# The operations of the attention and Fourier part in a written-out order

## The chip, the cores and the metric

The kernel runs on one core of a Trainium2 chip. The time is that of one execution on the device, in microseconds (us), measured without the profiler over several runs; their median counts. One more execution was recorded by the profiler, and all rows below are from it.

## The reference

For 8 batches of 8 heads, 576 positions and 64 features a head, a linear attention is computed without a softmax, then normalized; the result is reordered to `x` of 8 x 576 rows of 512. On `x` a layer follows that mixes by Fourier transforms and has a feed-forward net.

```python
kv = np.einsum('bhsd,bhse->bhde', k, v)
out = np.einsum('bhsd,bhde->bhse', q, kv)
rms = np.sqrt(np.mean(out * out, axis=-1, keepdims=True) + 1e-06)
x = out / rms * g_norm                       # then heads side by side: (B, S, 512)
mixed = real(fft(fft(x, axis=1), axis=2))
u = x + mixed
un = (u - mean(u)) / sqrt(var(u) + 1e-06)
return u + np.maximum(un @ w_ch1, 0.0) @ w_ch2    # 512 -> 2048 -> 512
```

Input weights arrive in 64 bits and are converted on the chip.

## The kernel before

The program has two parts. The second, the larger share of the feed-forward net, is written in the order in which it runs and is not touched. The first part, up to some 330 us, does for each of the 8 batches: the products of k and v (`plan_kv`, L950: four operations of 24 matmul instructions each, contraction over 96 rows into 64 columns of the array), transposes of q (`plan_q`, L1019: six operations of four transposes), the attention outputs (`plan_out`, L1046: three operations of 32 instructions, contraction over 64 rows, alternating between the upper and the lower half of the array), scaling and folding on the vector engines (`plan_y`, `plan_fold`, `plan_split`), the Fourier transform along the positions (`plan_seq`, L1280: four operations of seven matmuls of 290 columns) and along the features (`plan_chn`, L1324: six operations of four fp32 matmuls of 130 columns), and transposes of u (`plan_turn`, L1422: six operations of four transposes). Beside these it converts the first weights (`plan_w`), and for blocks of 512 rows it does the first slices of the feed-forward net (`plan_early`): three first products (L726, 12 matmuls of 512 columns each) with ReLU into a high half h on ScalarE (L736) and a low half on VectorE (L739), then four second products (L744, nine matmuls each).

Matmuls of L726, L744 and L1280 are fp32r; transposes, L1324, L950 and L1046 are fp32.

Each of these pieces is registered as an operation (`op`, `dma`) with an engine, an estimated cost, a rank, the operations that it needs and the buffers that it takes. There are 1,715: 398 on TensorE (PE), 451 on VectorE (DVE), 429 on ScalarE (ACT), 212 on GpSimd (POOL), 220 loads and stores on SyncE (SP), and a few markers. Buffers come from rings of fixed size (`RINGS`), among them 8 PSUM banks (`p8`), 6 half tiles of h and 6 tiles for k and v.

`Plan.run` is a list scheduler. It plays the operations through with the estimated costs; whenever an engine is free it takes the ready operation of the lowest rank whose buffers are free. `shift` first adds an offset from the table `SHIFT` to each rank. `pin` chains each engine's instructions in the order found, up to 300 us of planned time.

Of the kernel before, what the change touches and what calls it, by code (L numbers as in the profile page):

```python
# [54 lines left out]
SHIFT = {  # L55
    ("", "DVE", -100): -2880.5,
    ("", "POOL", -40): -937,
    ("", "SP DMA", -40): -23730.5,
    ("", "HOST", 0): -1181.5,
    ("", "POOL", 10): 24,  # L60
    ("", "SP DMA", 10): 294.5,
    ("", "POOL", 20): 552.5,
    ("", "SP DMA", 20): -63868.5,
    ("", "POOL", 30): 1213.5,
    ("", "POOL", 40): 1162.5,
    ("", "POOL", 50): 2073,
    ("", "POOL", 60): 3539,
    ("", "POOL", 70): 6370.5,
    ("", "DVE", 85): -240,
    ("", "PE", 85): 1946,  # L70
    ("", "SP DMA", 85): 991.5,
    ("", "HOST", 9000): 139.5,
    ("chn", "ACT", -34): 315,
    ("chn", "DVE", -34): 25,
    ("chn", "PE", -34): 3750.5,
    ("chn", "SP DMA", -34): 18885,
    ("chn", "ACT", 16): 1136,
    ("chn", "DVE", 16): 22530.5,
    ("chn", "PE", 16): 7,
    ("chn", "POOL", 16): -981.5,  # L80
    ("chn", "SP DMA", 16): -292,
    ("chn", "ACT", 26): 3465.5,
    ("chn", "DVE", 26): 18.5,
    ("chn", "PE", 26): -28.5,
    ("chn", "SP DMA", 26): -1643.5,
    ("chn", "DVE", 36): 36.5,
    ("chn", "PE", 36): -334.5,
    ("chn", "POOL", 36): -148,
    ("chn", "SP DMA", 36): -641.5,
    ("chn", "ACT", 46): 72966,  # L90
    ("chn", "DVE", 46): 404.5,
    ("chn", "PE", 46): -656,
    ("chn", "POOL", 46): 769,
    ("chn", "SP DMA", 46): 2653,
    ("chn", "ACT", 56): -555,
    ("chn", "DVE", 56): -1076,
    ("chn", "PE", 56): 57521.5,
    ("chn", "POOL", 56): -191.5,
    ("chn", "SP DMA", 56): -527,
    ("chn", "ACT", 66): -18.5,  # L100
    ("chn", "DVE", 66): 19,
    ("chn", "PE", 66): 259.5,
    ("chn", "POOL", 66): -733.5,
    ("chn", "SP DMA", 66): -1681.5,
    ("chn", "ACT", 76): 28.5,
    ("chn", "DVE", 76): 521,
    ("chn", "PE", 76): 1380.5,
    ("chn", "POOL", 76): -141,
    ("chn", "SP DMA", 76): 1068,
    ("dft", "POOL", -37): -79,  # L110
    ("dft", "SP DMA", -37): -552.5,
    ("dft_d", "ACT", -35): -1247.5,
    ("dft_d", "DVE", -35): 2333.5,
    ("dft_d", "POOL", -35): -601,
    ("dft_rest", "POOL", 9): 1006,
    ("dft_rest", "SP DMA", 9): 7159,
    ("dft_split", "ACT", -37): 22716,
    ("dft_split", "POOL", -37): 1615,
    ("dft_split", "ACT", 9): 73006,
    ("dft_split", "POOL", 9): -14.5,  # L120
    ("early", "ACT", -100): -25,
    ("early", "DVE", -100): 2547,
    ("early", "SP DMA", -100): 400,
    ("early", "PE", 1000): 43.5,
    ("early", "PE", 1010): 3621,
    ("early", "PE", 1030): 720,
# [72 lines left out]
    ("out", "PE", 62): 1265.5,
    ("out", "POOL", 62): -863.5,  # L200
    ("out", "PE", 72): -402.5,
    ("out", "POOL", 72): 2316.5,
    ("q", "ACT", -39): 70,
    ("q", "PE", -39): -2780,
    ("q", "POOL", -39): 1767,
    ("q", "PE", 11): 936.5,
    ("q", "POOL", 11): 250.5,
    ("q", "ACT", 21): -440,
    ("q", "PE", 21): -816,
    ("q", "POOL", 21): 2781,  # L210
    ("q", "ACT", 31): -127.5,
    ("q", "PE", 31): 3763.5,
    ("q", "POOL", 31): -635,
    ("q", "ACT", 41): 143.5,
    ("q", "PE", 41): -179,
    ("q", "POOL", 41): 154,
    ("q", "ACT", 51): 1602,
    ("q", "PE", 51): 620.5,
    ("q", "POOL", 51): 4526.5,
    ("q", "ACT", 61): 3768.5,  # L220
    ("q", "PE", 61): 1082.5,
    ("q", "POOL", 61): -550.5,
    ("q", "ACT", 71): 924,
    ("q", "PE", 71): 4825,
    ("q", "POOL", 71): 54,
    ("q_load", "SP DMA", -39): -23057.5,
    ("q_load", "SP DMA", -38): -28773.5,
    ("q_load", "SP DMA", 11): -1479.5,
    ("q_load", "SP DMA", 21): 1231,
    ("q_load", "SP DMA", 31): 8702,  # L230
    ("q_load", "SP DMA", 41): 19825,
    ("q_load", "SP DMA", 51): 22558,
    ("q_load", "SP DMA", 61): 68611,
    ("q_load", "SP DMA", 71): 72453.5,
    ("seq", "ACT", -35): -1889,
    ("seq", "DVE", -35): -198.5,
    ("seq", "PE", -35): 73,
    ("seq", "ACT", 15): -1912,
    ("seq", "DVE", 15): 1180.5,
    ("seq", "PE", 15): 29647,  # L240
    ("seq", "ACT", 25): 1319.5,
    ("seq", "PE", 25): -337,
    ("seq", "ACT", 35): -145,
    ("seq", "DVE", 35): 22658,
    ("seq", "PE", 35): -2808,
    ("seq", "ACT", 45): -1081,
    ("seq", "DVE", 45): -357.5,
    ("seq", "PE", 45): 650,
    ("seq", "ACT", 55): -516.5,
    ("seq", "DVE", 55): 377.5,  # L250
    ("seq", "PE", 55): 745.5,
    ("seq", "ACT", 65): -1914,
    ("seq", "DVE", 65): 22574,
    ("seq", "PE", 65): 6859,
    ("seq", "ACT", 75): 2415.5,
    ("seq", "DVE", 75): -676.5,
    ("spare", "DVE", -100): 119,
    ("spare", "PE", -100): -544,
    ("spare", "TICK", 0): 16,
    ("spare", "PE", 20000): -2023.5,  # L260
    ("split", "ACT", -36): 1252.5,
    ("split", "POOL", -36): -368,
    ("turn", "ACT", -33): 753,
    ("turn", "DVE", -33): 918.5,
    ("turn", "PE", -33): -632.5,
    ("turn", "ACT", 17): 1166.5,
    ("turn", "DVE", 17): -2156.5,
    ("turn", "PE", 17): -214.5,
    ("turn", "ACT", 27): 228,
    ("turn", "DVE", 27): 820.5,  # L270
    ("turn", "PE", 27): 842.5,
    ("turn", "ACT", 37): -1380.5,
    ("turn", "DVE", 37): -211.5,
    ("turn", "PE", 37): 1841,
# [84 lines left out]
class Plan:  # L359
# [81 lines left out]
    def run(self):  # L441
# [4 lines left out]
        users = {o.n: [] for o in self.ops}  # L446
# [1934 lines left out]
```

## Time and profile before

| what | value |
|---|---|
| median of 3 runs | 961.56 us (961.0 to 962.49) |
| the profiled execution | 962.68 us |
| its span, first to last instruction | 960.9 us |
| granted TensorE clock, mean | 1.00 |
| PE, DVE, ACT, POOL busy | 951.0, 683.9, 383.6, 443.7 us |

Busy times of PE are those of pipelined matmuls: a matmul's duration is longer than its distance to the next one, so costs are read from start to start. In the rows below a line with x24 merges 24 instructions; its first number is the first one's start, its second the time to the last one's end. PEld is the load of weights into the array.

### The profile page before, as it was taken

What the parts mean: (1) busy time and instruction counts of PE and PEld (TensorE: products, weight loads), DVE (VectorE), ACT (ScalarE), POOL (GpSimd) and SP (SyncE); (2) the same over time, 40 slices, a digit from 0 to 9 for tenths busy, and PEclk for the clock granted to TensorE, in tenths of its full rate; (3) what the DMA queues carried; (4) which work ended last, traced back from release to release, by engine and by line L of the source; (5) the groups of instructions that cost most, each with busy time, mean ns of one, the idle gap of its engine ahead of it and who ended that gap; (6) DMA issues with size and microseconds to landing.
All of it is one profiled execution on the core that took longest, in us unless ns stands there. A gap on an engine that the chain in (4) does not pass through costs nothing.

```text
span 960.9 us, 15968 instructions
## 1 busy us (share of the span) xinstructions
PE 951.0 (99%) x5934; PEld 799.0 (83%) x5934; DVE 683.9 (71%) x1199; ACT 383.6 (40%) x719; POOL 443.7 (46%) x436
## 2 busy tenths in 40 slices
PE   9999999999999999999999999999999999999998
PEld 7888889888888888888888888888888888888886
DVE  4889776678797478999457967586757685675554
ACT  2666766758655233433314321351225212521110
POOL 3557778676764215556725044825472437210000
PEclk9999999999999999999999999999999999999999
DMA  9999995955447899988489397529643675213412
GB/s 241 224 225 270 234 296 156 307 125 197 152 151 247 323 335 339 339 302 299 169 341 330 116 376 252 206 66 310 238 154 105 232 279 194 89 66 135 184 63 88
DMA packets 112654, 210.39 MB, mean 219 GB/s; under 512 B 45292, under 2 KB 66688, under 8 KB 103616
## 3 DMA queue, kind: packets, MB, share of 16 engines
q1 hardware_dynamic: 109536, 199.92, 63.1%
q0 software_dynamic: 1920, 6.29, 1.8%
q10 hardware_dynamic: 1120, 3.15, 1.1%
q8 instruction: 47, 0.77, 0.3%
q14 instruction: 31, 0.25, 0.1%
HBM read 141.40 MB, written 67.93 MB: 218 GB/s over the span
## 4 chain that ended last, share of the span: by engine, by line
PE 94%; DMA 2%; DVE 2%; issue 1%; SPq 1%; POOL 0%; ACT 0%; DVEq 0%; POOLq 0%
PE acc L2188 23%; PE ps_h L2153 20%; PE ps_h L1791 11%; PE acc L1802 10%; PE acc L744 8%; PE ps_h L726 7%; PE ps_f L1280 3%; PE ps_o L1046 3%; PE ps_f L1324 2%; PE ps_k L950 2%; PE ps_s L798 2%; DMA vm<-in_v_dram 2%; PE ps_t L1422 1%; PE ps_q L1019 1%; DMA km<-in_k_dram 1%
## 5 line engine op out<-in xcount | busy, mean ns | idle before, releaser
L2188 PE MATMUL acc<-w2c,hh 128*128 128x512 f32 x640 | 197.7, 390 | 0.0
L739 DVE SCALAR_TENSOR_TENSOR hl<-ps_h,hh 128x512 fp32r<-128x512 f32 x144 | 98.5, 687 | 103.6 <-ACT hh L736 103.2
L736 ACT ACTIVATE hh<-ps_h 128x512 fp32r<-128x512 f32 x144 | 85.8, 597 | 216.4 <-PE ps_h L2153 89.9
L2188 PEld LDWEIGHTS acc<-w2c,hh 128*128 128x128 f32 x640 | 119.7, 188 | 25.4
L2198 DVE TENSOR_TENSOR us<-acc,us 128x512 f32<-128x512 f32 (+1 forms) x161 | 106.9, 681 | 42.3 <-PE acc L2188 41.9
L2188 PE MATMUL acc<-w2c,hl 128*128 128x512 f32 x320 | 124.5, 389 | 0.0
L2153 PE MATMUL ps_h<-t,w1c 128*128 128x512 f32 x480 | 115.3, 389 | 0.0
L2153 PEld LDWEIGHTS ps_h<-t,w1c 128*128 128x128 f32 x480 | 90.1, 188 | 18.7
L1824 POOL TENSOR_TENSOR us<-us,low 128x512 f32<-128x512 f32 x30 | 45.6, 1524 | 99.3 <-ACT low L1821 93.4
L2153 PE MATMUL ps_h<-b,w1c 128*128 128x512 f32 x360 | 91.2, 389 | 0.0
L2153 PEld LDWEIGHTS ps_h<-b,w1c 128*128 128x128 f32 x360 | 67.6, 188 | 14.0
L2188 PEld LDWEIGHTS acc<-w2c,hl 128*128 128x128 f32 x320 | 60.1, 188 | 12.4
L726 PE MATMUL ps_h<-unTh,w 128*128 128x512 f32 x216 | 67.6, 395 | 1.3 <-DVE hl L739 1.3
L744 PE MATMUL acc<-w,hh 128*128 128x512 f32 x216 | 67.8, 399 | 0.0
L1802 PE MATMUL acc<-w,hh 128*128 128x512 f32 x216 | 64.2, 390 | 0.0
L1791 PE MATMUL ps_h<-unTh,w 128*128 128x512 f32 x192 | 59.9, 393 | 0.0
L2019 POOL TENSOR_TENSOR z<-z,low 128x512 f32<-128x512 f32 x24 | 31.0, 1296 | 58.4 <-DMA low<-unT_scr 58.3
L1096 POOL TENSOR_TENSOR x<-x,gb 96x512 f32<-96x512 f32 (+1 forms) x36 | 46.1, 1302 | 10.6 <-ACT x L1063 10.4
L2170 DVE TENSOR_TENSOR ps_h<-ps_h,s 128x512 f32<-128x512 f32 x60 | 39.8, 693 | 13.8 <-PE ps_h L2153 13.2
L2255 ACT COPY s<-ps_h 128x512 f32<-128x512 f32 x20 | 11.7, 587 | 92.5 <-PE ps_h L2153 92.5
L726 PEld LDWEIGHTS ps_h<-unTh,w 128*128 128x128 f32 x216 | 39.7, 188 | 9.5 <-DVE hl L739 1.5
L1802 PEld LDWEIGHTS acc<-w,hh 128*128 128x128 f32 x216 | 40.5, 188 | 8.3
(207 smaller groups left out, 1969.1 us busy)
## 6 DMA issues: line engine op xcount, KB each, us to landing
w1c<-w_scr SPq DMA_DIRECT2D x13, 1792.0 KB
raw<-in_moe_w_ch_dram SPq DMA_DIRECT2D x32, 512.0 KB
w2c<-w_scr SPq DMA_DIRECT2D x14, 1024.0 KB
unT_scr<-unTh SPq DMA_DIRECT2D x9, 1024.0 KB
unT_scr<-unTl SPq DMA_DIRECT2D x9, 1024.0 KB
part_scr<-part SPq DMA_DIRECT2D x36, 256.0 KB
w_scr<-w1q SPq DMA_DIRECT2D x5, 1792.0 KB
km<-in_k_dram SPq DMA_DIRECT2D x29, 288.0 KB
```

The costliest lines, as they stand in the source:

```text
L726: nc.tensor.matmul(ps, w[c][:, kc * P : (kc + 1) * P], unT[a][:, kc, :], start=(idx == 0), stop=(idx == 3 * KC - 1),)
L736: nc.scalar.activation(hh, ps, AF.Relu)
L739: nc.vector.scalar_tensor_tensor(hl, ps, 0.0, hh.bitcast(F32), ALU.max, ALU.subtract)
L744: nc.tensor.matmul(acc, hpair[a][:, i * P : (i + 1) * P], w[c], start=(first and n == 0), stop=(last and n == 2),)
L1096: nc.gpsimd.tensor_tensor(v_, v_, gb[:n].unsqueeze(1).to_broadcast([n, H, D]), ALU.mult)
L1791: nc.tensor.matmul(ps, w1_of(f, c, kc), unTs[j][a][:, kc, :], start=(idx == 0), stop=(idx == 3 * KC - 1),)
L1802: nc.tensor.matmul(acc, hpair[a][:, i * P : (i + 1) * P], w2_of(f, c), start=(first_ and n == 0), stop=(last_ and n == 2),)
L1824: nc.gpsimd.tensor_tensor(ut, ut, part, ALU.add)
L2153: nc.tensor.matmul(ps, w[:, A_OF[m], c, kc * P : (kc + 1) * P], b[:, a, kc * BT : (kc + 1) * BT], start=(fresh and idx == 0), stop=(done a ...
L2170: nc.vector.tensor_tensor(to, a, b, ALU.add)
L2188: nc.tensor.matmul(ps, hpair[a][:, i * P : (i + 1) * P], w2c[n][:, r, c], start=(idx == 0), stop=(idx == 5),)
L2198: nc.vector.tensor_tensor(ut[:, cols], ps[:, cols], ut[:, cols], ALU.add)
```

## The change

The table `SHIFT`, the method `shift` and the list scheduler go. In their place stands the string `ORDER`: two characters, as digits in base 64, are the number of an operation, counted in the order of registration. `run` goes through the operations in this order, works out a planned time for each only to tell `pin` whether it lies before 300 us, takes buffers and emits. The costs, the dependences, the rings, `pin` and `PIN_UNTIL` stay. `plan_chn` gets one more argument: the additions onto x now wait in the plan for the reduction of x's first column (`zero`, L1156).

```diff
-SHIFT = {
-    ("", "DVE", -100): -2880.5,
...
-}
+ORDER = (
+    "000Z044-1a1n5u05065B0708091d0A0B0C030D0E0F1g1Z0G0H0I0J500K0L1j0M510N1c0O0P0Q0R0S0T0U520V0W0X1f0Y5354"
...
+    "PRPSQRPTPWPUPVPXPYPZPcPaPbPdPe"
+)
+DIGITS = "0123456789ABCDEFGHIJKLMNOPQRSTUVWXYZabcdefghijklmnopqrstuvwxyz+-"
...
+        digits = [DIGITS.index(c) for c in ORDER]
+        order = [self.ops[64 * a + b] for a, b in zip(digits[::2], digits[1::2])]
+        assert len(set(order)) == len(self.ops)
+        slots = {r: [0] * n for r, n in self.rings.items()}
...
+        for o in order:
+            t = max([0] + [a.done + (0 if a.eng == o.eng else self.HOP) for a in o.after]) + o.wait
+            t = max(t, free.get(o.eng, 0), port if o.port else 0)
+            for b in o.bufs:
+                if b.t is None:
+                    first = min(slots[b.ring])
+                    slots[b.ring].remove(first)
+                    t = max(t, first)
+                    b.t = b.make() or True
+            self.pin(o.emit, t)
...
-    def plan_chn(b, t, x, pt, dones):
+    def plan_chn(b, t, x, pt, dones, read):
...
-            adds = [op("DVE", 690, r, fn, pms, [x, pm], port=True) for fn in (add_l, add_r)]
+            adds = [op("DVE", 690, r, fn, pms + read, [x, pm], port=True) for fn in (add_l, add_r)]
...
-            adds = [op("POOL", 1240, r, fn, pms, [x, pm]) for fn in (add_l, add_r)]
+            adds = [op("POOL", 1240, r, fn, pms + read, [x, pm]) for fn in (add_l, add_r)]
...
-            plan_chn(b, t, xs[t], pt, pts)
+            plan_chn(b, t, xs[t], pt, pts, [zs[t]])
```

Decoded, PE's operations begin to differ at its 159th, at 87 us. The first 27 from there, by kind and number:

```
before: out540 kv665 q679 q681 q683 q686 first1442 seq447 kv668 seq448 kv671 seq452 kv674
        second1445 out711 second1448 q688 q690 seq453 out702 q832 q834 chn457 chn458 chn476 chn477 chn492
after:  q683 out540 kv665 q679 seq447 first1442 q681 q686 seq453 seq448 seq452 second1445 kv668 kv674 kv671
        chn457 out711 chn458 q690 q688 chn476 second1448 out702 out693 q836 chn477 second1451
```

## Rows read from the trace of the kernel before

**Rows 1.** The page: busy times, PE's slices, and the chain by engine.
```profile
PE 951.0 (99%) x5934; PEld 799.0 (83%) x5934; DVE 683.9 (71%) x1199; ACT 383.6 (40%) x719; POOL 443.7 (46%) x436
...
PE   9999999999999999999999999999999999999998
...
PE 94%; DMA 2%; DVE 2%; issue 1%; SPq 1%; POOL 0%; ACT 0%; DVEq 0%; POOLq 0%
```
**Rows 2.** Stretches: us; busy of PE, PEld, DVE, ACT, POOL; clock, DMA share, GB/s.
```profile
87.00:250.00 163.00, 161.24 (x1684) 142.05 (x1683) 113.23 (x241) 112.24 (x237) 121.55 (x135) 1.00 0.74 214
```
**Rows 3.** PE's waits, 84 to 335 us: total us, times, longest.
```profile
PE ps_h L726 <- DVE hl L739: 1.3, 1, 1.3
PE ps_k L950 <- DMA vm<-in_v_dram: 0.4, 1, 0.4
```
**Rows 4.** Stretch 87 to 250 us, line 1046 alone, then line 950 alone.
```profile
87.00:250.00 163.00, 25.15 (x512) 23.08 (x512) 1.00 0.74 214
87.00:250.00 163.00, 13.61 (x384) 12.12 (x384) 1.00 0.74 214
```
**Rows 5.** Timeline of PE, 102 to 106 us: start us, us, engine, line, form, count.
```profile
102.02 0.39 PE L744 MATMUL acc<-w,hl 128*128 128x512 f32 x1
102.34 1.57 PE L1046 MATMUL ps_o<-kvt,fq 64*96 64x64 f32 x32
103.84 0.73 PE L744 MATMUL acc<-w,hh 128*128 128x512 f32 x2
104.41 0.40 PE L744 MATMUL acc<-w,hl 128*128 128x512 f32 x1
104.65 0.62 PE L744 MATMUL acc<-w,hh 128*128 128x512 f32 x2
105.11 0.39 PE L744 MATMUL acc<-w,hl 128*128 128x512 f32 x1
```
**Rows 6.** Timeline of PE, 94 to 97 us: a kv product between whole work.
```profile
94.74 0.92 PE L950 MATMUL ps_k<-vm,km 96*64 96x64 f32 x24
95.59 1.07 PE L1280 MATMUL ps_f<-cs,xhl 128*128 128x290 f32 x6
96.50 0.29 PE L1280 MATMUL ps_f<-css,xst 98*128 98x290 f32 x1
```
**Rows 7.** Timeline of PE, 106 to 108 us: transposes, then L1280.
```profile
106.02 0.82 PE L1019 MATMUL ps_q<-ident,qt 96*128 96x96 f32 x8
106.63 1.06 PE L1280 MATMUL ps_f<-cs,xhl 128*128 128x290 f32 x6
107.53 0.30 PE L1280 MATMUL ps_f<-css,xst 98*128 98x290 f32 x1
```
**Rows 8.** Timeline of PE, 119 to 126 us: transposes and kv products.
```profile
119.85 0.83 PE L1422 MATMUL ps_t<-ident,x 96*128 96x96 f32 x8
120.61 1.62 PE L950 MATMUL ps_k<-vm,km 96*64 96x64 f32 x48
122.16 0.88 PE L1422 MATMUL ps_t<-ident,x 96*128 96x96 f32 x8
122.96 0.92 PE L950 MATMUL ps_k<-vm,km 96*64 96x64 f32 x24
...
124.86 0.96 PE L1280 MATMUL ps_f<-cs,xhl 128*128 128x290 f32 x6
125.65 0.30 PE L1280 MATMUL ps_f<-css,xst 98*128 98x290 f32 x1
```
**Rows 9.** Timeline of PE, 215 to 219 us: two outputs in a row.
```profile
215.19 2.96 PE L1046 MATMUL ps_o<-kvt,fq 64*98 64x64 f32 x64
218.08 0.73 PE L726 MATMUL ps_h<-unTh,w 128*128 128x512 f32 x2
```
**Rows 10.** Timeline of ACT at 100 us: the copy of a batch's kv sum.
```profile
100.19 0.37 ACT L961 COPY kvt<-ps_k 128x256 f32<-128x256 f32 x1 [2.97 <-PE ps_k L950]
```
**Rows 11.** Timeline of DVE at 138 us: two folds.
```profile
137.73 2.63 DVE L1163 TENSOR_TENSOR ab<-x 96x256 f32<-96x256 f32 x6
```

More of the change, by code (lines that the diff above doesn't have):

```diff
@@ new lines @@
+ORDER = (
+    "000Z044-1a1n5u05065B0708091d0A0B0C030D0E0F1g1Z0G0H0I0J500K0L1j0M510N1c0O0P0Q0R0S0T0U520V0W0X1f0Y5354"
+    "1i551q561b1C5C1y575D0a580b4f1e595E0c5A1h025F2v2z2k0d2q1o5G1k1r5H1l0e1+0f5I1w4r0g1x0h0i1-0j201p0k5J0l"
+    "0m4g0n5K0o1z0p1m4h0q0r0s5h2M4i5i1s4j2P235k1t2Q2N24254k2S5l2T262O4l5n2R2f2e1u2g295o214m1v2h27222A5q4s"
+    "2i3G4t2E5r283H2B3J2C5v5j2H2D2K5m3I2U2I2V2F3K2W3L2L5p4u2X2G5w2J4v614n2a2Z3M2Y300t3N315s332b5t0u320v0w"
+    "2j0x4o2c0y0z4w0+4p342p0-10112d355x385z2w5y8B395-5+2+12603A13011436153B168C371718191A624q1B634x2l6N3C"
+    "4y2n8D2r3DF96O64FA66656R2-682m8K2x676G6P6S2o6Q2y4z2s6H693E6K6I3F6T6L8EFC6A1D8F8G6D1EFD8H1F6J6B8I6MFB"
+    "8JFF6E6C3O2t6FFG2u4+6U3P6V6WFI6X8L3ZFJ3c8M3a3b3Q6Y3d6ZCz3R6a3S6bFE3n3T3o6l6n1G7+3p1H6m6c7-6d6oFH6e3q"
+    "813r3s82476p3t3e6qFK3u6s6g6h48FL846i6r4N3U853v4O493V1I3w3f1J3X1K4A3W3g804B6k4C1L873z4D88423+1M3Y3h1N"
+    "4P8340435L4Q454R3j1O4S1P5X4F4T4I4G1Q6f864J4LAb6j1R3-3k1S4X414a444Y461T6t1U4H4b4d896u4K4M8A1V4ZAc5M1W"
+    "1X4cAN4e6v8k5NAO8l8N6w8P5O8m1YAjMS8o8n6x8p8O6y8q8Q5P3i8R8rMn5Q8bMT6zMU3l5R8cMVMo6+5S8d8f8e3m8g5Y8h8s"
+    "AQ5T5ZAhAR5U8SAiMWAT5V5W8TAPAU8W5aAd8U8a6-5b8XAWAeMXMY8Z5cAX8V3x8Y5d8t3yAf8u5e8iAkAg4E758vMZ4U5f8wMa"
+    "704VAl5g4W748x718jC+95Mb728z738y768+ASC-77AY999ACm78Mc94AV9BCn90Aa79MdAZ9198B7Cp9C9293Cq9H7ABBAoAm96"
+    "BC7S9E9GMeB8D69KApB99LAnBAAq9F7B9IBDA+Mf7D9J9M7CMgAr9DCs9N7UCtD4Av7T7FA-Mh7WD57VAw7EB2B07Y7iB17IAx7N"
+    "7LB5MiD07M7jD1MjD29P7XD3FNAsMk7QB67k7R7J7G7m9Q7K7O7H7a7lMl7d7Z7n9T7gFOAtMm7e7oCrAu7b7PCoB3Cv7cBFCu7p"
+    "7hB47q7v7s7rBH7y9OAy7t7zCwBG9UHY7uAz9SN8Ms9RBI9V7fBJ9WBKN9BMMvBLMtBNBUBYBaHZ9X7wBE7xD7HbCxD8BZBTBXHc"
+    "9Z8-MuBb9rCy9YHeBeBcMp9aMw9cHfBd9bBP9dMxBQ9eDWMqMr9fBV9hDa9gDBBRD9DbA6DAFVDD9sBfDXM-DCBjDY9kBkDZBgDc"
+    "BlA59tMyBmBh9v9iDe9jDNMzFMBiA7M+A8DE97A9DODdBOBW9uDRDSAAFTN0BoDTDI9lABFUBnBpDFDUFWBqDGFPBr9mDPDHBtDJ"
+    "9xDQFQAI9nDKDgFRBsBSFS9w9pDfN29qBuDhALBwDi9yBv9oN1DLA0HmN3CUA3BxDMA4ByBzAFFXB-CEA1ACB+CFCGADC09zAGCH"
+    "AEFvAMCWCIAJHnDVAH9+HdFw9-C1FxA2HgHaDjCJFyC2DsC3C4CVCKHhN5CYHiDlJxCXCLAKCaDkFaNVN6FYCMDmFZNGFzDnDwDy"
+    "F+FcCZC5C6DzNACbF-NHCcD-DoCdFbDpD+N4DqC7CNNWNDC8HuCOE2NIE3DtE4DuDxFmNEE7NFN7E5FdFnJyNBK8E1FqNCJ+HjFo"
+    "FuFhFpChJ-CeFiCPFeE6NSK1FrFtE0FsCfK2CSFfNJCTCgE8FjCQE9FgCiHvCjNKHqG3G1C9HwNLEBCCNTCDG2FkEACkG4ECCACl"
+    "CRNsHkG5EDEGHsHtNtEEG6CBEFG0HlEHGGHrNMEJFlEIGFNNG7HoG8EtGBIINOGCGHK0IJHpK3K4IKK5ILHzHxH+GIGEEdG9NPDr"
+    "DvGKGLGJGMH-GVEuNQNXGWNRGXNUEvGYIMK9ExEwEeEzEfINI0EhKAHyEgKHEiI9I4EyI5GNI6JzGOEjIOK6I1I2IPEKELI3EMNd"
+    "IAGDGPK7GSIDIEGRIFGQNaNeEOGTIBICGUENKFI7NfElGZEmEQKGEnGaNYEPNZEqGbKIGfGdKJIGERNbEaETESNcF1EWI8GeIREk"
+    "GcF2ITE+ErF3NgISE-GgEUF0GhEVGAEsNjNhEoEYNiEZIUIVIQEpEXODIXGiNkKDIWEbKhNlIfKEOEIYGkKiIkNpKjIHKlKkKmIi"
+    "KpKnF6NqKKEcGjKMGlKBKNKOGmIlNmKLGnIaImGoKCIeIbKYNnIcInNoIrKPKcGpKdKeH1KTPjIpGqNuIoGrKQKUNrKXKRPkKZKS"
+    "PxIqN+KVNvIsNwKaItF7KbKqNxIgIjF8KWPlN-PmIvKsKrH0O0IuNyHHH2KfGzNzIwGsH4HGG+O1IxGxHIG-GtH3GyIZHKH6PnO4"
+    "O2PoH5F4O3PpKtHJHDO5H8KuIzHMKvO6H7IyI+PqGvH9HLGwOAQSKwHAKgHNPrHOF5I-HQJ0J1HPHRKxO7HSL5L7GuHBK+KoHCIh"
+    "J2PsL1L2OFJ3L4J5L8KzLAKyK-LBJ4HELDOIIdO8LEO9LFL3OaOBLGObL9JfHTOJPtLCOLPuOGPyOKOCPvOHJhPwPzL6P+J6OMJQ"
+    "LIL0HUJPONLHJgJ7LJJjOOMKJRLKJiJTJkJ8HVJ9LRHWJAJSJBMLP-JCLMMMORQ0JlLNMNOPHXMOHFOQQ1JpOSJFJUQ2LLJKJqJI"
+    "MPJVJMQTLOLQOTQ3LPJrQfJsQ4OULSJDJGLUJEJtLTJWJLJHM2QUOVJXQVJcOWJYOXM4JaJmJbJnJZQWJoM3QXOYLVOfOZQYLXJd"
+    "QZQ5JJOxQaM6M5LWOgM8JuOyLYLpJvLZLoJeJNLbOcOhLqLsLaLrLuLcQbLdOiQcM7QdOdLtQgOeJOQeLvOjLeJwLlMHOkLmL-MC"
+    "M0LnLwOlLfM1MILzMJLjMDLxMEMFL+OoOmLyLgLhMGOnLkLiM9QhMAOpQiOqQjMBQkPIOrQlPJQmQ6OuQnQ7PfQ8Q9OvP0QAOsQB"
+    "OtOwQCPgQoQDOzPiPhQIP3O+P1P2O-QEMQP4P5QFP6MRQJQKP9QLP7P8PAPBPFPCPDPNQGPGPEQHPHPKPOPPQMQNPQQOPLPMQPQQ"
+    "PRPSQRPTPWPUPVPXPYPZPcPaPbPdPe"
+)
@@ L434, in pin @@
             self.last[i.engine] = i.name
-    def shift(self):
-        for o in self.ops:
-            stage = o.stage[len("plan_") :] if o.stage.startswith("plan_") else ""
-            o.rank += SHIFT.get((stage, o.eng + " DMA" * o.dma, round(o.rank)), 0)
     def run(self):
-        import heapq
-        self.shift()
-        users = {o.n: [] for o in self.ops}
-        need = {}
-        ready = {}
-        events = []
-        for o in self.ops:
-            need[o.n] = len(o.after)
-            for a in o.after:
-                users[a.n].append(o)
-        for o in self.ops:
-            if not o.after:
-                heapq.heappush(events, (0, o.n, "ready", o))
+        digits = [DIGITS.index(c) for c in ORDER]
+        order = [self.ops[64 * a + b] for a, b in zip(digits[::2], digits[1::2])]
+        assert len(set(order)) == len(self.ops)
+        slots = {r: [0] * n for r, n in self.rings.items()}
         free = {}
@@ L459, in run @@
         port = 0
-        cold = 0
-        left = len(self.ops)
-        t = 0
-        n = len(self.ops)
-        self.trace = []
-        while left:
-            if not events:
-                left = [o for o in self.ops if o.done is None]
-                raise RuntimeError(
-                    f"the plan is stuck at {t}: {self.rings}, "
-                    + str([(o.eng, o.rank, o.emit.__qualname__.split(".")[-3:]) for o in left[:8]])
-                )
-            t = events[0][0]
-            while events and events[0][0] <= t:
-                _, _, kind, o = heapq.heappop(events)
-                if kind == "ready":
-                    ready.setdefault(o.eng, []).append(o)
-                elif kind == "slot":
-                    self.rings[o] += 1
-            again = True
-            while again:
-                again = False
-                for eng, q in ready.items():
-                    if free.get(eng, 0) > t or not q:
-                        continue
-                    q.sort(key=lambda o: (o.rank, o.n))
-                    for o in q:
-                        want = {}
-                        for b in o.bufs:
-                            if b.t is None:
-                                want[b.ring] = want.get(b.ring, 0) + 1
-                        if o.port and port > t:
-                            continue
-                        if all(self.rings[r] >= c for r, c in want.items()):
-                            break
-                    else:
-                        continue
-                    q.remove(o)
-                    again = True
-                    for b in o.bufs:
-                        if b.t is None:
-                            self.rings[b.ring] -= 1
-                            b.t = b.make() or True
-                    self.pin(o.emit, t)
-                    cost = o.cost * (2 if eng == "PE" and cold > 0 else 1)
-                    cold -= o.dense
-                    self.trace.append((t, t + cost, eng, o))
-                    end = free[eng] = t + cost
-                    if o.port:
-                        port = end
-                        n += 1
-                        heapq.heappush(events, (end, n, "free", None))
-                    if o.dma:
-                        pipe = max(pipe, end + 1300) + o.lag
-                        free[eng] = max(end, pipe - self.AHEAD)
-                        end = pipe + 700
-                    for b in o.bufs:
-                        b.left -= 1
-                        b.close = max(getattr(b, "close", 0), end)
-                        if not b.left:
-                            n += 1
-                            heapq.heappush(events, (b.close, n, "slot", b.ring))
-                    n += 1
-                    heapq.heappush(events, (free[eng], n, "free", None))
-                    o.done = end
-                    for u in users[o.n]:
-                        need[u.n] -= 1
-                        if not need[u.n]:
-                            at = max(
-                                a.done + (0 if a.eng == u.eng else self.HOP) for a in u.after
-                            )
-                            n += 1
-                            heapq.heappush(events, (max(at, t) + u.wait, n, "ready", u))
-                    left -= 1
@@ new lines, in run @@
+        for o in order:
[8 more added lines that the diff above has]
+            self.pin(o.emit, t)
+            end = free[o.eng] = t + o.cost
+            if o.port:
+                port = end
+            if o.dma:
+                pipe = max(pipe, end + 1300) + o.lag
+                free[o.eng] = max(end, pipe - self.AHEAD)
+                end = pipe + 700
+            for b in o.bufs:
+                b.left -= 1
+                b.close = max(getattr(b, "close", 0), end)
+                if not b.left:
+                    slots[b.ring].append(b.close)
+            o.done = end
```

282 lines of the change are left out of this document (removed).

## The prediction

> **What bounds the kernel now.** I read the page's busy times and its chain first. The reader is to see there that TensorE (PE) is busy for 951 of 960.9 us and that the chain which ended last runs over PE for 94% of the span [rows 1]. The slices under it show PE at nine tenths or more up to the last one. Next came the stretches: from 87 to 250 us PE is busy 161.2 of 163 us, with the granted clock at 1.00, the 2.4 GHz level, while VectorE (DVE), ScalarE (ACT) and GpSimd (POOL) have 112 to 122 us each [rows 2]. So in the part that is reordered there are only two ways to save time: let PE do the same multiplications in less PE time, or take away the little that PE waits. Third, PE's waits between 84 and 335 us: two, 1.3 us for DVE's low half of h (L739) and 0.4 us for a load of v [rows 3], just what is missing in the stretch. Last, the timeline of PE at the edges between kinds of work, since a busy PE can hide lost time between two matmuls: start to start tells it.
>
> **What changes.** Decoding the list (two digits are one operation's number) gives SyncE's 220 operations in the same order as before, and PE's first 158, up to 87 us, in the same order. From there PE's 240 operations are the same ones in another order, and so are those of DVE, ACT and POOL. No instruction is added or taken away; the four new dependences on the three zero sums only affect when the planner thinks an operation runs. Two kinds of operation use half of the array: the kv products (L950, 96 rows by 64 columns) and the attention outputs (L1046, 64 rows). After 87 us there are 16 of each: 512 instructions at 32 each and 384 at 24 each [rows 4]. Before, the outputs stand in 15 runs and the kv products in 11, and these 26 runs make 24 blocks, since two outputs are directly followed by kv. In the list they are 11 and 8 runs, in 14 blocks. PE goes between whole, row-halved and column-halved work 49 times before and 33 times after.
>
> **What an edge costs.** An accumulating matmul (L744) is followed by the next one 0.23 us later (104.41 to 104.65), by an output 0.32 us later (102.02 to 102.34): entering a block costs 0.09 [rows 5]. Leaving it: the first two matmuls behind an output take 0.57 us to the third (103.84 to 104.41) where 0.46 is normal (104.65 to 105.11): 0.11 [rows 5]. Behind a kv product the six matmuls of L1280 take 0.91 (95.59 to 96.50) [rows 6] against 0.79 (124.86 to 125.65) [rows 8]: 0.12. Behind kv, eight transposes take 0.80 (122.16 to 122.96), behind whole work 0.76 (119.85 to 120.61), both with a kv product next: only 0.04 where fp32 work follows [rows 8]. Then there is a fixed part of each run: one kv product takes 0.85 to the next section's start [rows 6], two take 1.55 [rows 8], so 0.70 is the work and 0.15 is fixed; one output takes 1.50 [rows 5], two 2.89 (215.19 to 218.08) [rows 9], so 1.39 and 0.11.
>
> The Trainium skill says the same from the other side: TensorEngine Tiling (Array Packing), section Tiling Modes, has it that changing the tiling mode, unlike changing the tile, drains TensorE. The trace agrees: 0.09 on entering, and 0.04 to 0.12 after leaving. The page TensorE: Matmul & The Clock Gate, section Single matmul latency, puts a lone matmul 166 ns above its streaming time; as an estimate from that page, 16 drains fewer are 2.7 us, where the rows below give 3.0.
>
> **The sum on PE.** Four output runs fewer at 0.11: 0.44. Three kv runs fewer at 0.15: 0.45. Ten entries fewer at 0.09: 0.90. Exits: before, 6 of kv and 5 of outputs go into fp32r matmuls (6 x 0.12 + 5 x 0.11 = 1.27) and 13 into transposes (0.52), together 1.79; after, none of the 14 goes into fp32r work: 8 into transposes and 6 into the channel products (L1324), fp32 as well. I price those 6 like a transpose, the nearest row in kind: 14 x 0.04 = 0.56, so 1.23 less. Together 3.02 us less.
>
> Against it stands that the list chops whole work finer: sections of one kind grow from 124 to 158. Transposes followed by fp32r work: eight transposes take 0.61 (106.02 to 106.63) where 0.67 is normal (0.76 less the 0.09 of an entry), but the matmuls behind them 0.90 (106.63 to 107.53) instead of 0.79 [rows 7, 8]: 0.05 an edge. These go from 16 to 23: 0.35 more. Channel products followed by fp32r work go from 5 to 15; I take 0.02 for each, 0.20, between nothing and the 0.05 of transposes. Net: 3.02 - 0.55 = 2.47 us less PE time. Bounds: if leaving into channel products costs 0.12 and the other edge 0.05, 1.7 less; if the other edge costs nothing, 2.7 less.
>
> **The waits.** The 0.4 us for v stands before the second of four kv products at 97.2 us. In the list three of them come together behind three L1280 sections and the nine matmuls of an accumulation, at about 100 us, when that load has long landed. It goes. What is late next could be the output behind them: it needs ACT's copy of the kv sum, 0.37 us [rows 10], and only one channel product of four matmuls stands between. At most those 0.4 us are exposed, and the product covers most of them; I take nothing. The 1.3 us before the third first product of a block at 141 us was for DVE, which did two folds of three instructions (2.63 us) ahead of the low half of h that frees a PSUM bank [rows 11]. In the list that product stands right behind the one before it, and two banks are free then; this wait should go too. But banks get scarcer. Along the written orders, an operation that takes one of the 8 banks finds 3.5 free on average before and 2.4 after: two outputs in a row hold four banks until ACT and DVE have emptied them, and halves of channel products wait for their partners. I therefore let one wait of the known size, 1.3 us, come up elsewhere and count only the 0.44 as gained. Bounds: both waits gone and none new, 1.76 less; several of 1.3 us, below.
>
> The other engines' work is unchanged and hidden under PE [rows 2]. If that cover went at one place, the wait there would be of the order of one or two of DVE's instructions, as at 141 us. SyncE's order stays, so loads start where they did, except where one waits for a kv buffer that is freed up to 5 us later; a load that comes too late by this shows as another wait like the 0.4 for v, and is part of the range.
>
> Behind this part PE is full to the last slice [rows 1], so what PE gains before is gained in the whole. The profiled execution took 962.68 us (span 960.9 and 1.8 around): 962.68 - 2.47 - 0.44 = 959.8. The median of the three runs is 1.12 lower, so 958.7 there.
>
> **Rivals.** (1) Bank waits eat the gain. For it: 2.4 free banks instead of 3.5, and the one bank wait of the trace cost 1.3. Against it: the two outputs in a row that the trace has, at 215.19, are followed at once by a product [rows 9], and behind 141 us PE shows no wait at all. Two more waits of 1.3 than I count: 2.9 - 2.6 = 0.3 less, 961.3. (2) The same, at one place five times, ends slower: the list has five pairs of outputs where the old order had one. A pair fills four banks in 2.9 us, and ACT and DVE need longer to empty them. If behind each pair the next products find no bank, 5 x 1.32 = 6.6 us come in, against 2.47 + 1.76 saved: 2.4 slower, 963.9. It decides from 4.3 us of new waits. The Trainium skill warns of this in TensorEngine Tiling, section PSUM Bottleneck: tiling speeds up TensorE but not the emptying of PSUM; the trace shows no such wait behind its one pair. (3) No new wait and both old ones gone: 2.47 + 1.76 = 4.2 less, 957.3. (4) The list doesn't reach the chip as written: only operations that the planner puts before 300 us are chained. Half work ends at 245 us, so little speaks for it; about 961.5.
>
> **How the numbers follow.** Forecast 958.7 with 0.55; its own range, from the price of the fp32 exits and a wait of half the size, is 957.8 to 959.9. Rival (1) 0.22, (2) 0.08, (3) 0.10, (4) 0.05. A change under 0.2%, 1.9 us, can't be told from none here; the forecast of 0.3% is close to that line. Below 959.6 lie nine tenths of the forecast, rival (3) and a little of (1): 0.62. Slower than 963.5: 0.09. Within: 0.29. The range 957.0 to 961.8 holds the forecast, (3), (4) and most of (1).
>
> **What would show it.** Right: in the profile after, 11 runs of L1046 and 8 of L950 behind 87 us; an L1046 pair of about 2.9 us to the next section's start; transposes or channel products behind every block, 0.04 us slower than elsewhere; the start of the last matmul of L744 about 3 us earlier; the wait at 97 us gone. Wrong: PE waits on ACT or DVE instructions that read PSUM, together over 2.5 us between 87 and 330 us; a slower first section behind each block, which would mean that the edge moved and did not go; or the second part taking another time than before, which would mean that its order was changed too.

## The result and the profile after

The changed kernel is slower: 967.01 us median (965.42 to 967.49, 6 runs) against 961.62 (960.73 to 963.01, 6 runs) for the kernel before on the same chip, ratio 1.0052, 95% interval 1.0040 to 1.0065. The forecast was 958.7, with 961.8 as the upper end. The profiled execution took 966.54 us, its span 964.4.

The lines of code named here have moved up by 313: L1046 is L733 now, L950 is L637, L726 is L413, L744 is L431, L1280 is L967, L1324 is L1011, L1422 is L1109, L685 is L372.

The page of the kernel after, busy times and PE's slices, answers to [rows 1]:

```profile
PE 950.8 (99%) x5934; PEld 799.2 (83%) x5934; DVE 680.3 (71%) x1199; ACT 382.7 (40%) x719; POOL 444.8 (46%) x436
...
PE   9999999999998999999999999999999999999998
```

Its waits of PE from 84 to 335 us (total us, times, longest) answer to [rows 3]:

```profile
PE ps_w L372 <- POOL wp L368: 2.9, 1, 2.9
PE ps_f L967 <- DVE pm L1037: 1.0, 1, 1.0
PE ps_t L1109 <- DVE unTl L1121: 0.6, 1, 0.6
PE acc L431 <- DVE pt L993: 0.6, 1, 0.6
PE ps_o L733 <- ACT kvt L648: 0.5, 1, 0.5
```

Its stretches (us; busy PE, PEld, DVE, ACT, POOL; clock, DMA share, GB/s); the first answers to [rows 2]:

```profile
87.00:250.00 163.00, 162.50 (x1689) 144.40 (x1687) 113.53 (x247) 113.95 (x241) 121.69 (x138) 1.00 0.74 210
250.00:290.00 40.00, 37.78 (x230) 32.57 (x229) 36.76 (x85) 21.14 (x46) 24.46 (x24) 1.00 0.51 183
...
296.00:300.00 4.00, 1.06 (x6) 0.63 (x4) 1.30 (x2) 1.12 (x2) 3.40 (x5) 0.94 0.88 286
300.00:304.00 4.00, 4.00 (x14) 3.22 (x14) 3.51 (x6) 0.63 (x1) 1.28 (x1) 0.63 0.19 60
```

And the stretch of the kernel before that the prediction had not looked at:

```profile
250.00:290.00 40.00, 40.00 (x244) 35.00 (x243) 38.95 (x89) 22.34 (x50) 24.74 (x28) 1.00 0.51 175
```

The reader is to see three things. Up to 250 us the two old waits are gone and one of 0.5 is new. From 250 to 290 PE lost 2.2 of 40 us, in a stretch in which DVE had been busy for 38.95 of 40 before; it is busy for 36.76 now, so it isn't fuller than it was, but does its work in another order. And at 297 us there is a hole of 2.9 us, behind which the granted clock is 0.63. PE's timeline there, in the kernel after:

```profile
296.19 0.39 PE L413 MATMUL ps_h<-unTl,w 128*128 128x512 f32 x1
299.53 0.79 PE L372 MATMUL ps_w<-wp,mean_t 128*128 128x128 f32 x2 [2.94 <-POOL wp L368]
299.97 1.20 PE L413 MATMUL ps_h<-unTh,w 128*128 128x512 f32 x2
300.97 0.63 PE L413 MATMUL ps_h<-unTl,w 128*128 128x512 f32 x1
301.40 1.05 PE L413 MATMUL ps_h<-unTh,w 128*128 128x512 f32 x2
```

and POOL's beside it:

```profile
290.84 1.57 POOL L1053 TENSOR_TENSOR x<-x,pm 96x510 f32<-96x510 f32 x1 [8.46 <-DVE pm L1037]
292.36 1.19 POOL L1050 TENSOR_TENSOR x<-x,pm 96x514 f32<-96x514 f32 x1
293.50 1.19 POOL L1053 TENSOR_TENSOR x<-x,pm 98x510 f32<-98x510 f32 x1
294.65 1.19 POOL L1050 TENSOR_TENSOR x<-x,pm 98x514 f32<-98x514 f32 x1
295.80 0.47 POOL L366 TENSOR_TENSOR wp<-wa 128x128 f32<-128x128 f32 x1
296.22 1.18 POOL L1053 TENSOR_TENSOR x<-x,pm 96x510 f32<-96x510 f32 x1
297.35 1.19 POOL L1050 TENSOR_TENSOR x<-x,pm 96x514 f32<-96x514 f32 x1
298.49 0.99 POOL L368 TENSOR_TENSOR wp<-wp,wa 128x128 f32<-128x128 f32 x2
```

L366 and the two L368 are one operation, `w_sum_pool`: PE's L372 needs its sum. In ORDER it stands whole and ahead of these six additions. On the chip four additions run before it and two in its middle. So the list was not obeyed here. By the list's own planned times this operation starts at 305 us, behind 300, where `pin` chains nothing, and the framework's scheduler has put the additions in. The new `run` keeps strictly to the list and so plans later: its last PE operation starts at 366 us of planned time, that of the old planner at 349. Behind 300 us, and so unchained, are now 37 operations of PE, 59 of DVE, 46 of ACT and 10 of POOL; before they were 22, 38, 32 and 5.

**Where the time went.** The stage runs from the end of the common operations (before 87.16 us, after 85.90) to the second part's first matmul (344.13 and 347.66): 256.98 before, 261.76 after, +4.8. From there to PE's last end it is 613.1 in both. Waits: 5.65 less 1.76, +3.9. Slow clock: the twelve L413 behind the hole take 4.22 (299.97 to 304.19) instead of 2.72, and the L372 0.44 instead of 0.14, together +1.8. Edges: for each section of one kind I took its time to the next section's start, less its instructions times their steady distance, and averaged by neighbours; these sum to 8.6 us before and 6.6 after, -2.0, which is an estimate. The remaining +1.1 is what the other terms leave: stalls too short for a row of their own. The output pairs at 107 us (2.99) and 201 us (3.08), where 2.89 is normal, are 0.3 of it; where the rest lies, e1 and e3 tell in part.

PE reached the stage 1.26 us earlier than before, though nothing ahead of it has changed its order. Some of this is a gap at 38 us inside a kv product, in which PE waits for nothing that the profile shows: 1.08 us before, 0.65 after, and in the kernels below 0.8 to 1.2 with the old order and 0 to 1.3 with the new. It differs from program to program, so stages are compared below, not spans. The spans of the two profiled executions differ by 3.5 us (960.9 and 964.4): 4.8 less these 1.3. The medians differ by 5.4; the profiled execution of the kernel before, 962.68, was slower than its median.

### The profile page after: what moved, and what is told of

Same layout as the page of the kernel before. It is cut to its first block, busy times and chain, and to the rows that moved or that the text cites. A ratio compares the mean times of both kernels' runs of the same rounds, so it can differ in the third digit from the quotient of the medians.

```text
span 964.4 us, 15920 instructions
## 1 busy us (share of the span) xinstructions
PE 950.8 (99%) x5934; PEld 799.2 (83%) x5934; DVE 680.3 (71%) x1199; ACT 382.7 (40%) x719; POOL 444.8 (46%) x436
## 4 chain that ended last, share of the span: by engine, by line
PE 69%; DVE 1%; POOL 0%; SPq 0%; DMA 0%; issue 0%; ACT 0%; DVEq 0%
PE acc L1875 23%; PE ps_h L1840 20%; PE ps_h L1478 10%; PE acc L1489 10%; PE acc L431 3%; PE ps_h L413 2%; DVE unTl L1121 0%; PE ps_w L372 0%; SPq L1064 0%; DMA u_scr<-x 0%; DVE pm L1037 0%; PE ps_t L1109 0%; POOL x L1053 0%; DVE wp L358 0%; DVE ps_a L352 0%
## 5 line engine op out<-in xcount | busy, mean ns | idle before, releaser
L413 PE MATMUL ps_h<-unTh,w 128*128 128x512 f32 x216 | 68.7, 399 | 0.0
L431 PE MATMUL acc<-w,hh 128*128 128x512 f32 x216 | 67.0, 397 | 0.6 <-DVE pt L993 0.6
L916 POOL TENSOR_TENSOR xe<-ab 128x256 f32<-128x256 f32 (+1 forms) x42 | 31.0, 753 | 36.6 <-DVE ab L850 31.2
```

The costliest lines, as they stand in the source:

```text
L413: nc.tensor.matmul(ps, w[c][:, kc * P : (kc + 1) * P], unT[a][:, kc, :], start=(idx == 0), stop=(idx == 3 * KC - 1),)
L431: nc.tensor.matmul(acc, hpair[a][:, i * P : (i + 1) * P], w[c], start=(first and n == 0), stop=(last and n == 2),)
```

## Experiments

Theory T: the loss is in the unchained tail. Rival U: the written order itself is bad in its late part, where DVE is full. Both turned out to hold a share. "Stage" is measured as above, from one profiled execution; "waits" are PE's in it. The experiments ran in three sets, e1 to e4, e5 to e8 and e9 to e11, each with the kernel before beside it; its medians there were 962.23 (33 runs), 961.81 (23) and 962.05 (23). The ratios compare within a set; a difference of two medians of different sets is less sure by some 0.6 us, as the medians of the kernel before show.

| kernel | median us | ratio to before, 95% | stage | waits |
|---|---|---|---|---|
| before | 961.62 | | 256.98 | 1.8 |
| after | 967.01 | 1.0040 to 1.0065 | 261.76 | 5.7 |
| e1_pin_all | 962.55 | 0.9991 to 1.0012 | 257.03 | 2.7 |
| e2_old_list | 962.10 | 0.9991 to 1.0012 | 256.44 | 1.3 |
| e3_hybrid | 959.72 | 0.9967 to 0.9985 | 254.81 | 1.5 |
| e4_before_early | 961.75 | 0.9988 to 1.0006 | 256.49 | 1.3 |
| e5_pool_chained | 964.06 | 1.0009 to 1.0027 | 258.54 | 3.8 |
| e6_one_op | 966.17 | 1.0022 to 1.0050 | 259.29 | 4.8 |
| e7_ungrouped | 964.68 | 1.0019 to 1.0037 | 259.69 | 1.6 |
| e8_two_waits | 959.93 | 0.9957 to 0.9980 | 255.59 | 1.5 |
| e9_less_dve | 960.66 | 0.9975 to 0.9996 | 255.42 | 1.5 |
| e10_before_less_dve | 961.69 | 0.9990 to 1.0007 | 256.50 | 1.3 |
| e11_two_waits_less_dve | 958.87 | 0.9954 to 0.9979 | 254.09 | 0.5 |

**e1_pin_all: the whole list chained.**

```diff
-PIN_UNTIL = 300000
+PIN_UNTIL = 400000
```

> Edit: the changed kernel with PIN_UNTIL = 400000 instead of 300000, so that every operation of the list is chained in the written order; in the changed kernel the last 37 operations of PE, 59 of DVE, 46 of ACT and 10 of POOL are planned behind 300 us and are ordered by the framework's own scheduler (22, 38, 32 and 5 in the kernel before). Theory T (the chain ends too early for the new list): PE's wait of 2.9 us at 299.5 us for POOL's w_sum_pool (L368) goes, because w_sum_pool then stands whole and ahead of the additions on POOL, and with it the 3.4 us at a granted clock of 0.5 behind it (about 1.6 us): 967.0 - 2.9 - 1.6 = 962.5, between 961.5 and 963.5. Rival U (the written order itself is short of DVE between 255 and 300 us, where PE waits three times in the chained part, 2.2 us together): the lost time comes back as a wait for DVE at another place, 966 to 967.5. The three chained waits at 255, 274 and 283 us stay under both.

Measured 962.55, as T had it. POOL of this kernel:

```profile
290.31 0.47 POOL L366 TENSOR_TENSOR wp<-wa 128x128 f32<-128x128 f32 x1 [8.32 <-DVE wa L1159]
290.85 0.99 POOL L368 TENSOR_TENSOR wp<-wp,wa 128x128 f32<-128x128 f32 x2
291.80 1.17 POOL L1053 TENSOR_TENSOR x<-x,pm 96x510 f32<-96x510 f32 x1
```

`w_sum_pool` is whole, ahead of the additions, and done 7.6 us earlier; the hole and the slow clock are gone. So 4.5 of the 5.4 us lost (4.9 by the two ratios) are the tail that was not chained. But the written order, obeyed to the end, is still no faster than before: its stage is 257.03.

**e2_old_list and e4_before_early: the means, without the new order.** In e2 the digits of ORDER are those of the old planner's order, chained to the end. In e4 the kernel before stops chaining earlier:

```diff
-PIN_UNTIL = 300000
+PIN_UNTIL = 286817
```

> Edit: the changed kernel with the old order of operations, as the old planner found it, written out in ORDER, and PIN_UNTIL = 400000. This takes the list alone, without the grouping. Theory T: the list in itself costs nothing; 961.6 as before, between 960.8 and 962.4, with the waits of before (1.3 for hl at 141 us, 0.4 for vm at 97 us). Rival U: the same. Rival V (the way of writing the order, or chaining to the end, costs by itself): 964 or more.

> Edit: the kernel before with PIN_UNTIL = 286817 instead of 300000, so that as many operations of PE are left unchained as in the changed kernel: 37 (DVE 55, ACT 45, POOL 10). Nothing else differs. Theory T: the framework's scheduler then mixes matmuls of several operations and puts POOL's w_sum_pool elsewhere, and PE waits for DVE or POOL at 280 to 300 us: slower than before by 1 to 4 us, 962.6 to 965.6. Rival U: the end of the chain does not matter, 961.6 within 0.4.

e2 shows that writing the order out and chaining it to the end costs nothing. One thing in its expectation did not come: the wait of 0.4 for v. It is missing in e4 and e10 too, which also have the old order, so it came and went without the change; the stages of these three, 256.44 to 256.50, are the fairer measure of the old order than 256.98. e4 is a miss for T: 961.75, no loss. As many of PE's operations were left free as in the changed kernel; the scheduler mixed matmuls of different operations here too, but it put `w_sum_pool` ahead of the additions, and no wait came of it. So a chain that ends early is no loss by itself. It leaves the order to the scheduler, and the new order lost there.

**e3_hybrid: grouping with the old tail.** The new order up to PE's operation 320, about 245 us, then what is left in the order of before, all chained.

> Edit: the new order up to PE's operation 320 of 398 (about 245 us: all half-array work is done there), and the operations left in the order of before; PIN_UNTIL = 400000. Theory T: the grouping keeps its gain when the tail is a good one. Edges between kinds of work, summed over the trace of the changed kernel from 86 us to the first L1478, are 2.1 us less than before; the two waits of before (1.76) are gone, two new ones are there (0.5 at 101.9 us, 0.3 hidden in two output pairs): 961.6 - 2.1 - 1.76 + 0.8 = 958.5, between 957.5 and 960. Rival U (grouping pushes work of DVE late, whatever the tail): waits for DVE come at the seam or behind it, 961 to 966.

959.72: faster than before, the whole interval of the ratio lies below 1. The stage is 2.2 us shorter than before and 1.6 to 1.7 shorter than in e2 and e4; edges sum to 6.4 against 8.6, -2.2. Without any sum of edges, the stage less its waits is 253.3 against 255.2 before and 255.1 in e2, so 1.8 to 1.9 less. The grouping does what it says. T's 958.5 was 1.2 too low, mostly for a wait of 0.98 that came up at the seam (DVE's hl, at 246 us). The late part of the new order, about 245 us on, costs 962.55 - 959.72 = 2.8; by the stages it is 2.2, of which 1.2 are waits and 1.0 stalls too short for a row.

**e5_pool_chained and e6_one_op: is it that one operation?** e5 chains POOL alone beyond 300 us. e6 moves one operation in the list of e1.

```diff
-            if i.engine not in self.pinned or now > PIN_UNTIL:
+            if i.engine not in self.pinned or now > PIN_UNTIL + 1e5 * (i.engine == mybir.EngineType.Pool):
```

```diff
 POOL's operations in ORDER (e6_one_op)
-w1700 chn1416 chn1381 chn1380 chn1400 chn1415 chn1399
+chn1416 chn1381 chn1380 chn1400 w1700 chn1415 chn1399
```

> Edit: the changed kernel with POOL alone chained in the written order beyond 300 us of planned time; PE, DVE, ACT and SP stay as they were. Theory T (the loss is the one operation w_sum_pool, three instructions that the framework's scheduler lets six additions of chn into and ahead of): POOL then runs L366 and L368 as soon as DVE's wa is there (292.75 us in the changed kernel, so done by 294.4), PE's L372 comes at 296.6 and finds it done; the wait of 2.9 and the slow clock behind it go: 962.5, between 961.7 and 963.5. Rival U (DVE's and PE's unchained orders cost as much by themselves): 964.5 to 967.

> Edit: the kernel that is chained to the end (e1_pin_all), with one operation moved in the list: POOL's w_sum_pool (three instructions, 1.5 us) behind four of the six additions that follow it, so about where it runs in the changed kernel. Theory T: it ends at about 298.3 instead of 291.8 us, PE's L372 comes at 295.7 and waits 2.6 us, and the granted clock falls to 0.5 for about 3.4 us behind the wait, which costs 1.6: 962.55 + 2.6 + 1.6 = 966.7, between 965.5 and 967.5. Rival C (a wait of this size does not bring the clock down): 965.1. Rival U (other work takes the place): 962.5 to 963.

e6 brings 3.6 of the 4.5 us back with one operation: 966.17, within T's range. Its profiled execution, the fastest of the five at 964.43, shows PE's wait, 2.09 us:

```profile
298.95 0.49 PE L372 MATMUL ps_w<-wp,mean_t 128*128 128x128 f32 x2 [2.09 <-POOL wp L368]
```

e5 lies between both theories, at 964.06. `w_sum_pool` is done by 294.3 us as expected and its wait is gone; this is some 3.0 of the 4.5. The rest goes with the order that the scheduler gave the other engines' tails: PE's waits in e5 have new lines beside those of e1:

```profile
PE ps_t L1109 <- POOL x L1050: 1.0, 1, 1.0
...
PE ps_t L1109 <- DVE hl L426: 0.4, 1, 0.4
```

**e7_ungrouped: the price of an edge.** In e3's list 16 whole-array operations move into the blocks, as here into three kv products:

```diff
-kv821 kv818 kv824 turn505 turn502
+kv821 turn505 kv818 turn502 kv824
```

> Edit: e3_hybrid with the half-array work taken apart again: in 16 of its 18 places where two half-array operations follow each other, one whole-array operation (transposes or a channel product) from behind the block is put between. The other engines' lists and the tail stay. Theory T (edges are what the grouping saves): by the prices of edges summed over the trace, 10.4 us of edges instead of 6.4: 959.7 + 4.0 = 963.7, between 962.5 and 965.5, with no wait of note. Rival W (the gain of e3_hybrid over the kernel before comes from its waits and from an earlier start of the stage, not from edges): 959.7 to 961.

964.68, 5.0 more than e3. The timeline of e3_hybrid, where the three products and eight transposes take 2.91 (120.29 to 123.20):

```profile
120.29 2.32 PE L637 MATMUL ps_k<-vm,km 96*64 96x64 f32 x72
122.54 0.88 PE L1109 MATMUL ps_t<-ident,x 95*128 95x95 f32 x8
123.20 1.05 PE L967 MATMUL ps_f<-cs,xhl 128*128 128x290 f32 x6
```

and that of e7_ungrouped, 3.61 (120.80 to 124.41) for the same instructions:

```profile
120.80 0.92 PE L637 MATMUL ps_k<-vm,km 96*64 96x64 f32 x24
121.65 0.65 PE L1109 MATMUL ps_t<-ident,x 95*128 95x95 f32 x4
122.23 0.92 PE L637 MATMUL ps_k<-vm,km 96*64 96x64 f32 x24
123.08 0.55 PE L1109 MATMUL ps_t<-ident,x 96*128 96x96 f32 x4
123.56 0.92 PE L637 MATMUL ps_k<-vm,km 96*64 96x64 f32 x24
124.41 1.07 PE L967 MATMUL ps_f<-cs,xhl 128*128 128x290 f32 x6
```

0.35 for each of the two splits; over the whole stage 4.9 for 16, 0.31 each, with waits of 1.6 against 1.5. T holds, though 4.0 were priced for the 16; W falls.

**e8_two_waits: taking away what is left in e3.**

```diff
-PE:  kv671 chn457 out711 chn458      ACT: chn1090 folds1210 early1532
+PE:  kv671 chn457 chn458 out711      ACT: early1532 chn1090 folds1210
```

> Edit: e3_hybrid with two operations moved, one for each wait that PE has left in it: the output at 102 us one channel product later (behind the second chn of four matmuls, 0.45 us, so that ACT's copy of the kv sum is done), and ACT's ReLU of the first product that ends at 243.3 us ahead of a copy and a conversion (1.15 us with their own waits) that stand before it. Theory T: the waits of 0.50 (ACT kvt) and 0.98 (DVE hl) go and nothing is late next: 959.7 - 1.4 = 958.3, between 957.8 and 958.9. Rival: what stands behind them was waiting too and takes their place, 959.3 to 960.

The rival was right: 959.93, the same as e3. Both waits are gone, and three others stand behind 250 us in their place, 0.26, 0.26 and 0.76. PE came earlier to a stretch in which it then had to wait for DVE and POOL.

**e9, e10 and e11: DVE as the bound from 250 to 290 us.** Six of DVE's instructions are left out, 4.3 us by their shortest times; in e1's trace, where some take longer, they are 5.2:

```diff
-lambda n=n: w_steps(raw.t, ps.t, pf.t, high.t)[n]()
+lambda n=n, m=d.n: m in (1649, 1651, 1662, 1664, 1695, 1697) or w_steps(raw.t, ps.t, pf.t, high.t)[n]()
```

> Edit: e1_pin_all (the new order, chained to the end) with six of DVE's instructions left out: two of the four steps that turn 64-bit weights into floats (L352 and L358, 0.73 us each), for the three weights that DVE converts between 247 and 291 us; these weights come out wrong, all else is computed. That is 4.3 us less on an engine that is busy for 97% of 250 to 290 us in every kernel. Theory D (DVE is the bound of this stretch; PE's three waits there, 0.59 for unTl, 1.02 for pm and 0.56 for pt, are DVE being late): they go but for some 0.2, 962.55 - 2.0 = 960.6, between 960.0 and 961.3. Rival (they are the length of chains from PE over ACT, DVE and POOL back to PE, which a less busy DVE does not shorten): 962.0 to 962.8.

> Edit: the kernel before with the same six instructions of DVE left out (L665 and L671 there). A control for e9_less_dve: DVE is busy for 39.0 of the 40 us from 250 to 290 here too, but PE waits nowhere in them. Theory D: nothing to be gained, 961.8 within 0.6. Rival (less work of DVE makes the rest faster by itself): under 961.0.

> Edit: e8_two_waits with the same six instructions of DVE left out. In e8_two_waits PE came to the stretch 1.4 us earlier than in e3_hybrid and gave it back in three waits, 0.26 for POOL's x, 0.26 for DVE's unTl and 0.76 for DVE's x0l, between 252 and 269 us. Theory D: 0.3 to 1.3 of them go: 959.9 - 1.0 = 958.9, between 958.3 and 959.6. Rival (the waits are chains): 959.7 to 960.3.

All three came out where D had them: 960.66, 961.69 and 958.87. By the stages less work for DVE is worth 1.6 us in the new order (255.42 against 257.03) and 1.5 in e8 (254.09 against 255.59), and nothing in the order of before (256.50 against 256.44 in e2). By the medians it is 1.9 and 1.1, but these are of different sets, and the intervals of e8 and e11 to the kernel before lie almost upon each other: that e11 is faster than e8 rests on one trace of each. One figure in the expectation is wrong: 97% is DVE in the order of before. In e1_pin_all it is busy for 36.49 of the 40 us, 91%. So DVE bounds this stretch by what it does when, not by its sum. PE's waits in e9:

```profile
PE ps_f L967 <- DVE pm L1037: 1.0, 1, 1.0
PE ps_o L733 <- ACT kvt L648: 0.5, 1, 0.5
```

Of the three behind 250 us the waits for unTl and pt went; the 1.0 for pm stayed, where D had it go too. The trace of e9 shows what stands ahead of it:

```profile
268.45 0.36 ACT L1028 COPY me<-ps_f 96x258 f32<-96x258 f32 x1
270.70 0.47 DVE L1037 SCALAR_TENSOR_TENSOR pm<-ps_f,sgn_t,me 96x258 f32<-96x258 f32 x1
271.19 0.17 DVE L1294 COPY x0t<-x 34x8 f32<-34x8 f32 x1
...
272.10 1.28 DVE L1299 CAST x0h<-x 128x16 fp32r<-128x16 f32 x1
...
273.88 0.88 DVE L1037 SCALAR_TENSOR_TENSOR pm<-ps_f,sgn_t,me 96x258 f32<-96x258 f32 x2
```

ACT's copy for this channel product is done at 268.81. DVE combines the one half at 270.70 and the other, whose end frees the bank, only at 273.88 (the first of the two in the last row): between them stand the copies and casts of one other operation, 2.7 us, which the plan has at 0.8. In ORDER it stands between the two halves (`chn1261 p0_in1428 chn1260`); in the order of before the halves are neighbours. None of the instructions left out stands there. So this wait too is the order of DVE's list; no run put it right. The gain of 1.6 in the stage is the other two waits, 1.2, and shorter stalls.

## Why the prediction was wrong, step by step

- Runs and edges, right. Behind 86 us the trace has 11 runs of L733 and 8 of L637 as decoded. The forecast net of 2.47 came out at 2.0 in the changed kernel and 2.2 in e3 by the sum of edges, 1.9 in e3 by its stage less waits. Priced from single rows [rows 5, 6, 8], a split was 0.15 fixed, 0.09 to enter, 0.04 to leave; e7 measured 0.31.
- The waits named, half right: those for vm and hl [rows 3] are gone. Only the 1.3 for hl is the list's doing; the 0.44 for vm, which the forecast counts as its gain on waits, was missing in e2, e4 and e10 too, with the old order. "I take nothing" for the output behind three kv products was wrong by 0.5: the copy itself takes 0.38, but ACT did another one of 0.59 first and began it at 101.48, when the channel product that was to cover it (100.73, 0.69 us) had run out.
- "I therefore let one wait of the known size, 1.3 us, come up elsewhere": it was 2.7 in the chained part, which is also over the 2.5 that the prediction gave as a sign of being wrong, and not for banks behind pairs of outputs (rival 2: none stands behind one) but, apart from the 0.5, at 255, 274 and 283 us. **This step failed first**: "The other engines' work is unchanged and hidden under PE [rows 2]". Rows 2 end at 250 us, where the half-array work ends, but the list reorders everything up to some 330. Behind 250 DVE was full, 38.95 of 40 us, and PE had no wait only in the old order: e1 and e3, which differ from 245 us on, have waits of 2.2 and none behind 250. With the tail chained, the 2.2 and the short stalls give back what the edges gained (stage 257.03), so the forecast would have failed without the tail as well. The Trainium skill says in Perfetto Trace Analysis, section Optimization Strategy, that the most contended engine can change over time, and that gaps are to be read within a regime. The rows above agree: DVE is busy for 113.23 of the 163 us up to 250, and for 38.95 of the 40 behind.
- Rival 4 got the mechanism and the wrong price: "Half work ends at 245 us, so little speaks for it; about 961.5". **This step cost most**, 4.5 us. It asked what of the half-array work lies behind the end of the chain, not what else does: 37 of PE's operations and 10 of POOL's, `w_sum_pool` among them. Nor did it work out the planned times of the new `run`, though the diff showed that they would be new. The runs have in its place one operation taken apart on POOL, a wait of 2.94 us on PE and 1.8 us of slow clock behind it.
- The second part, unchanged: right, 613.1 in both.

The sum as it should have been, on the profiled executions' stages: edges -2.0, waits -1.76 + 2.7 + 2.94, slow clock +1.8, short stalls +1.1: +4.8.

Not settled: why the scheduler chose this order for POOL and a harmless one in e4; what the short stalls behind 245 us are, 1.0 us in the chained order; and whether a better late part exists than that of before. e11 suggests that some 1 us more is to be had if DVE had less to do between 250 and 290 us; with all the work done, e3_hybrid and e8_two_waits are the best found, 0.2% to 0.3% faster than before.

## What to carry to other kernels

Read the stretches over everything that a change reorders, not only over what it is meant for: an engine at 70% of the whole can be at 97% for 40 us, and there another order of its work can give a gain on another engine back. Where an order is enforced only up to a limit, work out what lies behind the limit with the new order's times, and look at the order that the chip ran. Part the two halves of such a change, here the grouped early part and the reordered late part: one of them was worth keeping.

## What the runs showed of the hardware

A hole in PE's work can cost more than itself. Up to 296 us the clock was granted in full, the 2.4 GHz level; PE did nothing for 2.94 us, and the L413 behind it ran at the 1.2 GHz level, 1.20 and 1.05 us a pair instead of 0.62, until 302.7. It doesn't come each time: of the six runs after, the one with a mean clock of 1.000 took 965.42, the five with 0.998 took 966.54 to 967.49. In e6, with a wait of 2.09 in the execution profiled, that one kept a clock of 1.000 and took 964.43; one with 0.999 took 965.05, and the three with 0.997 or 0.998 took 966.17 to 966.54. Without the hole, none of the eleven runs of e1 lies below 0.999. So a hole of 2 to 3 us brought some 1.7 us more in most executions, and none in others.

Such executions are not the hole's alone. Of the 79 runs of the kernel before in the three sets, whose longest wait in the profiled stage is 1.3 us, 23 have a mean clock of 0.998 or less, with medians of 963.5 to 963.7 against 961.7 to 961.8 for the others; no trace caught where their clock fell. None of the eleven runs of e3 has it, so part of the 2.5 us between the medians of the two is this: against the others of that set, 961.7, e3 is 2.0 faster. The Trainium skill describes the consequence in TensorE: Matmul & The Clock Gate, section HAM oscillation — how this bites in real kernels: the work that follows an idle gap runs at half the clock. The timeline above agrees; the profiled execution of e6, at a granted clock of 1.00 behind 2.09 us, doesn't.
